# Two further products of the second layer divided once more: a plan of 80 steps on eight banks, with its sums on three engines and DMA

## The chip, the cores and the metric

The kernel runs on one core of a Trainium2 chip. Its time is the device time of one execution in microseconds (us). The core has TensorE (PE, matmuls; PEld are its weight loads), VectorE (DVE), ScalarE (ACT), GpSimd (POOL) and SyncE (SP), each with a queue of its own that is worked off in order, and 16 DMA engines. SBUF is the core's working memory. TensorE writes its results to PSUM, 128 partitions by 8 banks of 512 fp32 numbers; GpSimd and DMA work on SBUF alone here.

## The reference

A causal convolution over 7 tokens with softmaxed weights for each of 8 heads, then a two-layer network with hardswish between its layers:

```python
def _attn_ref(x, weight):            # x: (8, 4096, 192), weight: (8, 7)
    w = np.exp(weight - np.max(weight, axis=-1, keepdims=True))
    w = w / (np.sum(w, axis=-1, keepdims=True) + 1e-09)
    ...
    out = np.einsum('hk,bskhg->bshg', w, x_unf)
    return out.reshape(B, S, D).astype(np.float32)

def _moe_ref(x, w_in, w_out):        # (32768, 192), (192, 2048), (2048, 192)
    h = x @ w_in
    relu6 = np.clip(h + 3.0, 0.0, 6.0)
    g = h * relu6 / 6.0
    return (g @ w_out).astype(np.float32)
```

## The kernel before, in words

The 32,768 tokens are cut into 32 blocks of 1024, each in two halves of 512. A block passes through a convolution (one multiplication on ScalarE, six taps on VectorE, L917-925), the first layer (`first_layer`, L496) and the second (`second_layer`, L589). Block 0 is done in another way (L801-963); blocks 1 to 31 run in the loop at L970. The order of all instructions is written by hand: under `manual_schedule` each engine's queue holds them as the code issues them, and the framework adds the waits.

**First layer.** y is split into three parts, high, low and mix (`split_high`, `split_rest`), and a copy with its halves exchanged is made by six DMAs on SP (`swap_parts`). There are 16 units: for n below 8 group 0 reads the own parts, from 8 on group 1 reads the exchanged ones. `begin(n)` runs the high and low matmuls into a slot of two banks and has ScalarE multiply them by 4097; `end(n)` adds the mix matmuls, ScalarE's relu and VectorE's gate, and then the slot is free. Four slots serve in turn, so begin(n+4) needs gate n. Group 0 writes A11 and A22, group 1 A21 and A12: the four quarters of g, for 8 chunks of 128 rows of the hidden dimension. Taps stand between the gates.

**Second layer.** g @ w_out is one Strassen step over the quarters: seven products P1 to P7, each with a sum of quarters (S1 = A21 + A22, S2 = S1 - A11, S3 = A11 - A21, S4 = A12 - S2) and a sum of weights (T1 to T4). S2 and S1 lie over A11 and A21, S4 over S3. A product has 96 rows, three column groups of 32; TensorE works four such groups at once, and the kernel writes four streams of matmuls, one for each group. `put` books a matmul at its stream's clock, two steps for 512 columns, one for 256; `do(t, ...)` books any other instruction at step t; at the end all are sorted by t and issued. Of P1 and P5 the first two thirds (64 columns) are taken once more by Strassen, over halves of the chunks, of the columns and of the tokens: seven small products of four matmuls in stream 3, with sums Z1 to Z4 (`small_sums`) and weights `w_s` (`small_weights`), 28 steps where the plain form has 32; the last third is run plainly. In this text (n, k) is small product k of P n, or the copy or addition behind it, and Z4 2 is sum 2 for P4. A stream has 82 steps. Three of the four slots are used; the fourth takes begin(0) of the next block's first layer.

**Sums.** P1's Z sums are done by GpSimd during group 0 (L552), S3 by GpSimd and VectorE (L555), two pairs of S1 by DMAs that add in SBUF, issued by GpSimd (L557), the other pairs by VectorE; P5's Z sums by VectorE in A22's place; S2 and S4 by VectorE at step 38. Results c11, c21, c22, c12 are put together on VectorE from PSUM (u3 = U2 + P7 and c21 = u3 + P4 among them), transposed there and stored by SP; c22 and c12 come out at the start of the next block (`finish`). The last block ends with its own order by halves of tokens (`end_lower`, `end_upper`).

Of the kernel before, what the change touches and what calls it, by code (L numbers as in the profile page):

```python
# [8 lines left out]
ALU = mybir.AluOpType  # L9
# [12 lines left out]
HIGH, LOW, MIX = range(3)  # L22


@with_exitstack
def kernel(
# [17 lines left out]
    G = 2  # L44
# [75 lines left out]
    w_s = cst.tile([P, 2, 4, NP // 2, QS], F32, name="w_s")  # L120
# [245 lines left out]

    new_results()
# [34 lines left out]
    def g_sums(engine, which, slots, width):  # L402

        forms = {
            3: (S3, A11, A21, ALU.subtract),
            2: (S2, S1, A11, ALU.subtract), 4: (S3, A12, S2, ALU.subtract),
        }
        for n in which:
            o, a, b, op = forms[n]
            for p in slots[::width]:  # L410
                r = slice(p, p + width)
                engine.tensor_tensor(out=o[:, r], in0=a[:, r], in1=b[:, r], op=op)  # L412
# [75 lines left out]
    y_own, y_other, pools, s1 = [], [None], [], []  # L488

    def swap_parts():  # L490
        y_other[0] = pools[0].tile([P, 3, K3, N], F32, name="y_other", tag="other")
        for n in range(3):
            swap(y_other[0][:, n], y_own[n])


    def first_layer(i, jobs):  # L496
# [6 lines left out]
        def mms(n, part, start=False, stop=False):  # L503
            group, c = divmod(n, NP)
            for s in range(K3):
                for k in range(2):
# [3 lines left out]
                        rhs=r32(y_other[0][r, part, s] if group else y_own[part][r, s]),  # L510
# [30 lines left out]
        for n in range(count):  # L541
# [7 lines left out]
            if n == 1:  # L549
                s1.append(ot.tile([P, NP, N], F32, name="s1", tag="shared")[:])  # L550
            if n < NP and n % 2:
                small_sums(s1[-1], A11, (1, 2, 3, 4), nc.gpsimd, every[n - 1 : n + 1])  # L552
            if n > NP and n % 2:
                pair = slice(n - NP - 1, n - NP + 1)
                g_sums(nc.gpsimd if n + 1 < count else nc.vector, (3,), range(NP)[pair], 2)  # L555
                if n + 3 < count:
                    nc.gpsimd.dma_start(out=S1[:, pair], in_=A22[:, pair], accum_op=ALU.add)  # L557
        for pair in (slice(NP - 2, NP), slice(NP - 4, NP - 2)):
            add(S1[:, pair], A21[:, pair], A22[:, pair])
# [20 lines left out]
    def small_weights(to, w):  # L580

        b11, b12, b21, b22 = (
            w_out[:, c::2, w, q * QS : (q + 1) * QS] for c in range(2) for q in range(2)
        )
        t1, t2, t3, t4 = (to[:, n] for n in range(4))
        for o, p, q in ((t1, b12, b11), (t2, b22, t1), (t3, b22, b12), (t4, b21, t2)):
            nc.gpsimd.tensor_tensor(out=o, in0=p, in1=q, op=ALU.subtract)

    def second_layer(i, between):  # L589
        last = i + 1 == NB  # L590
        ours = [free_slots.pop(0) for _ in range(3)]
        d, e, b, x_, a, c = (psum[:, 2 * n + k] for n in ours for k in range(2))
        ends = [psum[:, 2 * free_slots[0] + k] for k in range(2)] if last else [b, b]
        s5 = A22
        copy = nc.scalar.copy
        m = slice(0, DH)
        lo, hi = halves
        both = nc.sync, nc.scalar
        B, C, V = (bank[rows(3)] for bank in (x_, d, b))
        A, E = e[rows(3)], a[rows(3)]  # L600
        first, second, third, fourth = (rows(q) for q in range(4))
        late = {}
# [17 lines left out]
        def plain(j, bank, n, q, chunks, start=False):  # L620
            x, w = prod[n]
            x = S3 if x is None else x
            for k, ch in enumerate(chunks):
                put(j, 2, lambda ch=ch, k=k: matmul(
                    j, bank[rows(j)], w_out[:, ch, w, q * QS : (q + 1) * QS], x[:, ch],
                    start and k == 0,
                ))

        def small(n, m_, out, start=False):

            x, w = prod[n]
            sums, ws = (s1[-1], w_s[:, 0]) if n == 1 else (s5, w_s[:, 1])
            x11, x12, x21, x22 = four_parts(x)
            z1, z2, z3, z4 = four_parts(sums)
            b11, b12, b21, b22 = (
                w_out[:, h::2, w, q * QS : (q + 1) * QS] for h in range(2) for q in range(2)
            )
            t1, t2, t3, t4 = (ws[:, k] for k in range(4))
            xm, wm = {
                1: (x11, b11), 2: (x12, b21), 3: (z4, b22), 4: (x22, t4),  # L640
                5: (z1, t1), 6: (z2, t2), 7: (z3, t3),
            }[m_]
            for u in range(NP // 2):
                put(3, 1, lambda u=u: matmul(
                    3, out[:, lo], wm[:, u], xm[:, u], start and u == 0
                ))

        def plain_by_halves(j, n, q, t):
            w = prod[n][1]
            for ch in every:  # L650
                put(j, 1, lambda ch=ch: matmul(
                    j, ends[t][rows(j), halves[t]], w_out[:, ch, w, q * QS : (q + 1) * QS],
                    S3[:, ch, halves[t]], ch == 0,
                ))

        def tiles():
            new_results()
            if last:
                xts.insert(0, NP - 1)
            late.update(zip(("p7", "p5", "u3"), (results[0][m, n] for n in range(3))))  # L660

        for q in range(NQ):
            plain(q, d, 4, q, every, True)
            before = (1, 6, NP)[q]
            plain(q, c, 7, q, every[:before], True)
            plain(q, e, 1, 2, range(5 + q, 6 + q))
            do(clock[q], copy, out=e[rows(q + 1)] if q < 2 else p1[third], in_=e[rows(q)])
            plain(q, c, 7, q, every[before:])
            plain(q, a, 2, q, every[:6], True)
            plain(q, b, 6, q, every)  # L670
            plain(q, a, 2, q, every[6:])
            if last:
                plain_by_halves(q, 3, q, 0)
                plain_by_halves(q, 3, q, 1)
            else:
                plain(q, b, 3, q, every)

        def level_two(n, p, chunks, order):
            chunks, first_fill = list(chunks), [True]
            left = [list(chunks) for _ in halves]  # L680

            def fill_half(t, k):
                for _ in range(k):
                    ch = left[t].pop(0)
                    x, w = prod[n]
                    put(3, 1, lambda ch=ch: matmul(
                        3, (ends[0], x_)[t][fourth, halves[t]], w_out[:, ch, w, 2 * QS : 3 * QS],
                        x[:, ch, halves[t]], ch == 0,
                    ))

            def fill(k):
                plain(3, b, n, 2, [chunks.pop(0) for _ in range(k)], first_fill.pop() if first_fill else False)

            steps = {
                1: lambda: copy(out=B[:, lo], in_=A[:, lo]),
                2: lambda: copy(out=p()[first, lo], in_=A[:, lo]),
                6: lambda: copy(out=C[:, lo], in_=B[:, lo]),
                5: lambda: copy(out=p()[second, lo], in_=E[:, lo]),
                7: lambda: add(p()[second, hi], C[:, lo], p()[second, lo]),
# [319 lines left out]
```

## Time and profile before

| what | value |
|---|---|
| runs before | 2228.01, 2227.44, 2227.94 us; median 2227.94 |
| profiled execution, span | 2224.9 us |
| chain that ended last | PE 99%: second layer (L615) 49%, first layer (L508) 46% |
| DMA | 166.57 MB, mean 75 GB/s |
| gates (L306, 128x1024) | x496, 1219 ns each |
| relu (L302, 128x1024) | x496, 1113 ns each |
| 4097 multiplication (L520) | x465, 1008 ns each |
| taps (L921, 128x1536) | x186, 1802 ns each |
| S1 pairs by DMA (L557) | x62, 512 KB each, 5.0 us to landing |

The span counts from the first to the last instruction of one profiled execution; times are of other executions, without a profile. A row of a group gives the line, the engine, the operation, what it writes and reads, the count, the busy time and the mean of one. The chain is followed back from the last instruction, at each step to what released it. A windows row gives a stretch, its length, the busy time of each engine with the count of instructions, TensorE's granted clock (1.00 is full), the DMA engines' busy share and their GB/s. A timeline row gives start, duration, engine, line and operation, and in brackets how long the engine was idle before it and what ended that.

### The profile page before, as it was taken

How to read it: one execution, taken by the hardware profiler on the slowest of the kernel's cores; microseconds unless marked ns; L12 is line 12 of the kernel's file. 1: busy time of each engine (PE TensorE's matmuls, PEld its weight loads, DVE VectorE, ACT ScalarE, POOL GpSimd, SP SyncE). 2: the span in 40 equal slices, each digit the busy share in tenths (PEclk: the TensorE clock that was granted, in tenths of full speed). 3: DMA queues.
4: the chain of work that ended last, by engine and by line, in shares of the span. 5: the costliest groups of instructions: out<-in, count | busy, mean ns of one | idle time of the engine just before them, and what ended most of it. 6: DMA issues, size and time to landing. Idle time of an engine off the chain costs nothing.

```text
span 2224.9 us, 50339 instructions
## 1 busy us (share of the span) xinstructions
PE 2218.0 (100%) x21496; PEld 1532.7 (69%) x21496; DVE 1894.3 (85%) x1673; ACT 1379.2 (62%) x1678; POOL 823.8 (37%) x690
## 2 busy tenths in 40 slices
PE   9999999999999999999999999999999999999999
PEld 5467776677766777766777667776677776677766
DVE  8888888888888888888888888888888888888876
ACT  7457665576655676555766557665567655576654
POOL 2344432344422444223443234442244422344323
PEclk9999999999999999999999999999999999999999
DMA  6244224443244342344422444324434234442232
GB/s 157 57 98 85 49 58 91 85 83 62 53 82 91 77 80 47 71 91 84 85 48 58 91 87 81 67 49 82 91 79 81 47 67 91 84 84 52 55 77 34
DMA packets 253584, 166.57 MB, mean 75 GB/s; under 512 B 208017, under 2 KB 213137, under 8 KB 253361
## 3 DMA queue, kind: packets, MB, share of 16 engines
q1 hardware_dynamic: 234872, 129.46, 28.4%
q0 software_dynamic: 17248, 33.64, 8.7%
q8 instruction: 168, 2.75, 0.5%
q14 instruction: 56, 0.45, 0.1%
q10 hardware_dynamic: 1240, 0.27, 0.1%
HBM read 31.72 MB, written 25.17 MB: 26 GB/s over the span
## 4 chain that ended last, share of the span: by engine, by line
PE 99%; DVE 0%; DMA 0%; ACTq 0%; issue 0%; DVEq 0%; ACT 0%
PE psum L615 49%; PE psum L508 46%; PE psum L296 2%; PE psum L341 2%; DMA x<-in_x_dram 0%; DVE y L255 0%; DVE top L175 0%; ACTq L89 0%; PE psum L816 0%; DVE results L456 0%; DVE scale L171 0%; DVE y L251 0%; DVE scale L192 0%; DVEq L1014 0%; DVE results L462 0%
## 5 line engine op out<-in xcount | busy, mean ns | idle before, releaser
L615 PE MATMUL psum<-g,w_out 128*32 128x512 f32 (+1 forms) x6712 | 967.5, 552 | 0.0
L306 DVE SCALAR_TENSOR_TENSOR g<-g,psum 128x1024 f32<-128x1024 f32 (+1 forms) x528 | 618.3, 1186 | 198.8 <-ACT g L302 194.5
L578 POOL TENSOR_TENSOR s<-g 128x256 f32<-128x256 f32 x248 | 273.6, 1103 | 1241.1 <-DVE g L306 1200.5
L302 ACT ACTIVATE g<-psum,half 128x1024 f32<-128x1024 f32 (+1 forms) x528 | 564.8, 1087 | 6.0 <-PE psum L508 5.2
L615 PEld LDWEIGHTS psum<-g,w_out 128*32 128x32 f32 x6712 | 371.8, 110 | 246.0 <-issue 126.7
L508 PE MATMUL psum<-y,w_in 64*128 64x512 f32 x4464 | 521.4, 388 | 0.0
L508 PE MATMUL psum<-y_other,w_in 64*128 64x512 f32 x4464 | 516.0, 386 | 0.0
L520 ACT ACTIVATE psum<-psum 128x1024 f32<-128x1024 f32 x465 | 469.0, 1008 | 50.7 <-PE psum L508 48.4
L508 PEld LDWEIGHTS psum<-y,w_in 64*128 64x128 f32 x4464 | 413.5, 184 | 115.7 <-issue 26.0
L508 PEld LDWEIGHTS psum<-y_other,w_in 64*128 64x128 f32 x4464 | 418.1, 184 | 87.8
L615 PE MATMUL psum<-s,w_out 128*32 128x512 f32 (+1 forms) x3272 | 465.5, 570 | 0.0
L921 DVE SCALAR_TENSOR_TENSOR y<-x,c_sb,y 128x1536 f32<-128x1536 f32 x186 | 335.2, 1802 | 2.6 <-ACT y L919 1.3
L412 POOL TENSOR_TENSOR s<-g 128x1024 f32<-128x1024 f32 x93 | 285.9, 3074 | 26.2 <-DVE g L306 26.2
L615 PE MATMUL psum<-g,w_s 128*32 128x256 f32 x1240 | 282.8, 379 | 0.0
L615 PEld LDWEIGHTS psum<-s,w_out 128*32 128x32 f32 x3272 | 154.3, 110 | 81.9 <-issue 49.4
L615 PEld LDWEIGHTS psum<-g,w_s 128*32 128x32 f32 x1240 | 136.4, 110 | 67.7
L412 DVE TENSOR_TENSOR s<-g 128x2048 f32<-128x2048 f32 (+1 forms) x93 | 181.3, 1977 | 1.1
L615 PE MATMUL psum<-s,w_s 128*32 128x256 f32 x744 | 170.7, 379 | 0.0
L578 DVE TENSOR_TENSOR g<-g 128x1024 f32<-128x1024 f32 x124 | 151.7, 1224 | 5.3
L412 DVE TENSOR_TENSOR g<-g 128x2048 f32<-128x2048 f32 x62 | 139.1, 2284 | 0.0
L612 ACT COPY psum<-psum 32x512 f32<-32x512 f32 x93 | 51.3, 551 | 135.4 <-PE psum L615 135.4
L456 DVE TENSOR_TENSOR results<-psum,results 32x256 f32<-32x256 f32 (+3 forms) x128 | 69.3, 541 | 50.9 <-issue 45.5
(91 smaller groups left out, 1299.5 us busy)
## 6 DMA issues: line engine op xcount, KB each, us to landing
y_other<-y SPq DMA_DIRECT2D x186, 384.0 KB, 5.1
g<-g POOLq DMA_DIRECT2D x62, 512.0 KB, 5.0
out_dram<-results SPq DMA_DIRECT2D x378, 64.0 KB, 2.0
x<-in_x_dram SPq DMA_DIRECT2D x53, 388.5 KB, 7.7
stage<-in_moe_w_in_dram SPq DMA_DIRECT2D x16, 192.0 KB, 4.5
stage<-in_moe_w_out_dram SPq DMA_DIRECT2D x8, 384.0 KB, 6.8
x<-in_x_dram SPq DMA_DIRECT2D x7, 384.0 KB, 8.4
x<-in_x_dram POOLq DMA_DIRECT2D x2, 388.5 KB, 5.4
```

The costliest lines, as they stand in the source:

```text
L296: nc.tensor.matmul(out=psum[:, b], lhsT=w[r], rhs=src, start=start, stop=stop, skip_group_check=onto,)
L302: nc.scalar.activation(r6, h, ACT.Relu, bias=half[:], scale=1.0 / 6.0)
L306: nc.vector.scalar_tensor_tensor(out=g_, in0=g_, scalar=1.0, in1=h, op0=ALU.min, op1=ALU.mult)
L341: lambda p=p: nc.tensor.matmul(out=bank[j * QS : (j + 1) * QS, tokens], lhsT=w_out[:, p, w, cols], rhs=x[:, p, tokens], start=(first and p ...
L412: engine.tensor_tensor(out=o[:, r], in0=a[:, r], in1=b[:, r], op=op)
L456: nc.vector.tensor_tensor(out=out, in0=x, in1=y, op=op)
L508: nc.tensor.matmul(out=psum[:, 2 * slots[n] + k], lhsT=r32(w_in_parts[part][r, c, s]), rhs=r32(y_other[0][r, part, s] if group else y_own[ ...
L520: nc.scalar.mul(both(n), both(n), 4097.0)
L578: engine.tensor_tensor(out=o, in0=p, in1=q, op=op)
L612: streams[3].append((t - 0.5, lambda: fn(*args, **kw)))
L615: nc.tensor.matmul(out=out, lhsT=w, rhs=x, start=start, stop=True, tile_position=(0, j * QS), skip_group_check=True,)
L921: jobs.append(lambda k=k: nc.vector.scalar_tensor_tensor(out=y[:], in0=x[:, :, k : k + N], scalar=c_sb[:, k : k + 1], in1=y[:], op0=ALU.mu ...
```

## The change

P4 and P7 get the second Strassen step too. The fourth column group (stream 3) now runs 28 small steps each of P1 and P7 and 24 of P5; stream 1 runs P4's 28 and the four of (5, 4), whose result lies aside. Every stream has 80 steps. All four slots are taken. Four steps that write other banks (the last chunks of P5 and P4, and (5, 4)) stand between P6 and P3, which go to the same bank b; in them ScalarE copies b for u3. P4's Z sums are formed with other signs, so that a copy and an adding DMA can make them.

A table, `PLAN`, says for each sum at which step it is issued, and by whom: V VectorE, G GpSimd, D an adding DMA that GpSimd issues after SP or ScalarE has written the first operand. Negative steps lie in the first layer: t belongs to unit int(t + 16). `TIMES` and `ADDS` hold the steps of the other operations. P4's sums lie in the place of the block's own y parts, P7's in that of the exchanged ones (`region`, `sums_in`), P5's where P1's were, and S4 lies over A12 and no longer over S3. Results and transposed results lie in chunks 2 to 7 of A22, so relu and gate of the next block wait for the stores that read there. One tap moves to step 17.3 of the second layer, and the others stand behind units 0, 3 and 11. The exchange of y moves from step 18 to step 64.6, high, low and mix from steps 13 and 15 to steps 46 to 53. Weight sums of four products instead of two are formed at the start by GpSimd. The last block's own order is gone; its stores go to two queues.

```diff
+PLAN = (
+    (-6.74, 'Z4', 1, 'V'),
+    (-6.3, 'S3', 0, 'G'),
+    (-5.2, 'Z4', 2, 'D'),
+    (-3.71, 'S1', 0, 'D'),
+    (-2.66, 'Z4', 3, 'D'),
+    (0.13, 'S3', 3, 'V'),
+    (0.24, 'S3', 1, 'G'),
+    (1.42, 'S3', 2, 'G'),
+    (1.46, 'Z7', 1, 'V'),
+    (2.38, 'Z7', 2, 'V'),
+    (2.47, 'S1', 1, 'D'),
+    (11.07, 'Z7', 3, 'D'),
+    (11.5, 'S1', 2, 'V'),
+    (19.55, 'Z4', 4, 'V'),
+    (22.16, 'Z7', 4, 'D'),
+    (27.2, 'S1', 3, 'V'),
+    (28.62, 'Z5', 3, 'D'),
+    (33.36, 'Z5', 1, 'V'),
+    (34.07, 'S2', 0, 'V', 4),
+    (37.56, 'Z5', 2, 'V'),
+    (41.9, 'Z5', 4, 'D'),
+    (46.42, 'S2', 2, 'V', 4),
+    (49.16, 'S4', 0, 'V', 4),
+    (59.87, 'S4', 2, 'V'),
+    (66.26, 'S4', 3, 'V'),
+)
+TIMES = {'c11': 38.42, 't11': 57.95, 'u3': 60.97, 'c21': 64.27, 't21': 77.97, 'conv6': 17.32, 'high': 46.36, 'low': 47.15, 'mix': 53.24, 'swap': 64.57, 'x': 45.83, 'conv0': 70.49, 'conv1': 70.67, 'a22': 47.43}
+ADDS = {(1, 7): (0, 'V'), (1, 3): (2.43, 'V'), (4, 7): (0.25, 'V'), (4, 3): (1.08, 'V'), (5, 7): (1.83, 'V'), (5, 3): (0.0, 'V'), (7, 7): (0, 'V'), (7, 3): (0, 'V'), (5, 4): (0, 'V'), 'u3': (0, 'G'), 'c22': (0, 'V')}
+CONV_UNITS = (0, 3, 11)
...
-            if n == 1:
-                s1.append(ot.tile([P, NP, N], F32, name="s1", tag="shared")[:])
             if n < NP and n % 2:
-                small_sums(s1[-1], A11, (1, 2, 3, 4), nc.gpsimd, every[n - 1 : n + 1])
-            if n > NP and n % 2:
-                pair = slice(n - NP - 1, n - NP + 1)
-                g_sums(nc.gpsimd if n + 1 < count else nc.vector, (3,), range(NP)[pair], 2)
-                if n + 3 < count:
-                    nc.gpsimd.dma_start(out=S1[:, pair], in_=A22[:, pair], accum_op=ALU.add)
-        for pair in (slice(NP - 2, NP), slice(NP - 4, NP - 2)):
-            add(S1[:, pair], A21[:, pair], A22[:, pair])
+                small_sums(sums[1], A11, (1, 2, 3, 4), nc.gpsimd, every[n - 1 : n + 1])
+            if n == NP - 1:
+                sums[4] = sums_in("own", "sums4")
+                copy_for_sums(sums[4], A22)
+            for t, what, k, by, *width in PLAN:
+                if t < 0 and int(t + count) == n:
+                    sum_of(what, k, by, *width)
+
+    def sum_of(what, k, by, width=2):
+
+        engine = {"V": nc.vector, "G": nc.gpsimd, "D": None}[by]
+        pair = slice(2 * k, 2 * k + 2)
...
+    def copy_for_sums(to, x):
+
+        for k in (1, 2, 3, 4):
+            o, p, q = plus_form(to, x, k)
+            if any(entry[1:4] == ("Z4", k, "D") for entry in PLAN):
+                nc.sync.dma_start(out=o, in_=p)
...
+    def sums_by_dma(to, x, n):
...
+        nc.scalar.mul(o, p, scale)
+        nc.gpsimd.dma_start(out=o, in_=q, accum_op=ALU.add)
...
     def second_layer(i, between):
         last = i + 1 == NB
-        ours = [free_slots.pop(0) for _ in range(3)]
-        d, e, b, x_, a, c = (psum[:, 2 * n + k] for n in ours for k in range(2))
...
+        ours = [free_slots.pop(0) for _ in range(4)]
+        a, A_, E_, C_, B_, b, d, c = (psum[:, 2 * n + k] for n in ours for k in range(2))
...
+        results_in_a22()
+        p7, p5, u3 = (A22[m, k] for k in range(2, 5))
...
+        most, rest = every[: NP - 2], every[NP - 2 :]
+        for q in (0, 2):
+            plain(q, a, 2, q, True)
+        plain(1, a, 2, 1, True, most)
+        plain(0, d, 1, 2, True)
+        do(clock[0], copy, out=b[third], in_=d[first])
+        plain(0, c, 5, 2, True, most)
+        for k in (1, 5, 6, 2, 0, 7, 3, 4):
+            if k:
+                small(1, 4, k)
+                do(33 if k == 2 else ends_at(4, k, clock[1]), step, 4, k)
+            else:
+                plain(1, a, 2, 1, chunks=rest)
+        plain(2, d, 4, 2, True, most)
+        plain(2, c, 7, 2, True)
+        do(clock[2] + 1, copy, out=p7[third], in_=c[third])
+        for q in range(NQ):
+            plain(q, b, 6, q)
+        plain(0, c, 5, 2, chunks=rest)
+        do(clock[0] + 1, copy, out=p5[third], in_=c[first])
+        small(1, 5, 4, aside)
+        do(clock[1] + 1, copy, out=p5[first, hi], in_=aside)
+        plain(2, d, 4, 2, chunks=rest)
+        for q in range(NQ):
+            plain(q, b, 3, q)
+
+        waiting = {(7, 5): TIMES["a22"], (7, 2): TIMES["a22"] + 0.1}
+        for n, k in (
+            [(1, k) for k in (1, 5, 6, 2, 7, 3)] + [(7, 1), (1, 4)]
+            + [(7, k) for k in (5, 6, 2, 7, 3)] + [(5, 1), (7, 4)]
+            + [(5, k) for k in (5, 6, 2, 7, 3)]
+        ):
+            small(3, n, k)
+            do(waiting.get((n, k), ends_at(n, k, clock[3])), step, n, k)
...
+        do(TIMES["c11"], lambda: copy(out=spare["own"][m], in_=b[m]))
+        do(TIMES["c11"] + 0.2, lambda: add(a[m], a[m], spare["own"][m]))
+        for t, what, k, by, *width in PLAN:
+            if t >= 0:
+                do(t, sum_of, what, k, by, *width)
         for t, job in between:
             do(t, job)
...
+        do(TIMES["t11"], lambda: store(i, a, 0, 0))
+        do(TIMES["u3"], lambda: either(u3, b[m], p7, ALU.add, "u3"))
+        do(TIMES["c21"], lambda: add(p7, u3, d[m]))
+        do(TIMES["c21"] + 2 if last else TIMES["t21"], lambda: store(i, p7, 1, 0))
...
-        free_slots.extend(ours[n] for n in (0, 2, 1))
-        if last:
-            end_upper()
+        free_slots.extend(ours[n] for n in (3, 0, 1, 2))
         return [lambda: finish(1), lambda: finish(0)]
```

`either` is an addition on VectorE, or for "G" a copy by ScalarE and an addition by GpSimd. `step(n, k)` is the copy (ScalarE) or addition (VectorE, k = 7 and 3) behind a small product. The small products of P1, P7 and P5 use the same four places in banks A_, E_, B_, C_ one after the other.

## The prediction

> **What bounds the kernel now.** I read the page first, then the chain of waits, then one block of two layers (first layer from 988.77 us, second from 1021.67 us) in the windows, the waits and the timelines of its engines.
>
> ```profile
> PE 2218.0 (100%) x21496; PEld 1532.7 (69%) x21496; DVE 1894.3 (85%) x1673; ACT 1379.2 (62%) x1678; POOL 823.8 (37%) x690
> ...
> 988.77 32.90 PE psum L508 x288
> 1021.67 35.47 PE psum L615 x216
> ...
> 1021.67:1057.14 35.47, 32.73 (x28) 1.00 0.59 119
> 988.77:1021.67 32.90, 25.93 (x23) 1.00 0.16 26
> ...
> DVE g L306 <- ACT g L302: 6.0, 7, 1.2
> ```
>
> TensorE is never idle: the chain is its two layers in turn, 32.90 + 35.47 = 68.37 us for each of 31 blocks. 35.47 us are 82 steps, so a step (256 columns on four column groups) is 0.4326 us. The next engine is VectorE: 25.93 + 32.73 = 58.65 us of 68.37; of the 9.7 us left, 6.0 are gates that wait for ScalarE's relu in the first layer, and can be used only by running late. So TensorE's count sets the time as long as VectorE's queue keeps its dates.
>
> **What the change takes away.** Two steps a block: 2 x 0.4326 = 0.865 us, 26.8 us over 31 blocks. The second layer becomes 80 steps, 34.6 us, the cycle 67.5 us. It has 216 matmuls for 192, but in the last block before, four 256-column matmuls follow each other every 0.21 us, so issuing them sets nothing.
>
> **What it adds, by engine.** VectorE per block: two Z4 and two Z7 sums (1.2 us each, the 128x1024 sums of L578), five more 32x256 additions (0.43); it loses two Z5 sums and u3 (0.69). That is +3.9, so 62.6 of 67.5 us. GpSimd: six more accumulating DMAs (1.20 each) and u3, 25.3 to about 34 us. ScalarE: four scalings of 128x1024 (1.0) and some nine copies (0.36), 42.7 to about 50 us. DMA: six accumulations and two copies of 512 KB more. Sums of busy time fit everywhere; what counts is VectorE's order.
>
> **VectorE's queue, followed by hand.** These rows give the prices, start to start.
>
> ```profile
> 1021.57 3.48 DVE L306 SCALAR_TENSOR_TENSOR g<-g,psum 128x1024 f32<-128x1024 f32 x3 [1.16 <-ACT g L302]
> 1025.08 1.31 DVE L412 TENSOR_TENSOR s<-g 128x1024 f32<-128x1024 f32 x1
> ...
> 1038.21 4.49 DVE L412 TENSOR_TENSOR g<-g 128x2048 f32<-128x2048 f32 x2
> ...
> 1017.74 1.20 POOL L557 DMA_DIRECT2D g<-g  x1 [0.30 <-POOL s L412]
> 1018.49 2.89 POOL L412 TENSOR_TENSOR s<-g 128x1024 f32<-128x1024 f32 x1
> 1021.67 1.20 POOL L557 DMA_DIRECT2D g<-g  x1 [0.30 <-POOL s L412]
> 1022.87 2.43 POOL L412 TENSOR_TENSOR s<-g 128x1024 f32<-128x1024 f32 x1
> ```
>
> The last gate ends 3.4 us into the second layer, and it is paced by ScalarE, so it will again. I count from there: 1.2 for a sum of 1024 elements, 2.2 for 2048, 1.75 for a convolution tap (1.7 for low and mix), 0.45 for a 32x256 addition, 0.7 for 96x512, 0.65 for a transpose.
>
> First, S3's last pair. VectorE's sum started at 1025.08, GpSimd's ended at 1025.30, and VectorE's ended 1.09 after that: one of them waits for the other. In the start-up the same shows the other way round:
>
> ```profile
> 89.08 1.76 DVE L937 TENSOR_TENSOR y<-y,y 128x1536 fp32r<-128x1536 f32 x1 [1.61 <-ACT y L474]
> 90.76 2.01 DVE L477 SCALAR_TENSOR_TENSOR y<-y,y 128x1536 fp32r<-128x1536 f32 x1
> ...
> 88.77 0.65 POOL L83 DMA_DIRECT2D x<-in_x_dram  x1
> 89.43 1.72 POOL L587 TENSOR_TENSOR w_s<-w_out 128x128 f32<-128x128 f32 x1
> 91.22 1.86 POOL L587 TENSOR_TENSOR w_s<-w_out,w_s 128x128 f32<-128x128 f32 x1
> 93.05 0.45 POOL L587 TENSOR_TENSOR w_s<-w_out 128x128 f32<-128x128 f32 x1
> ```
>
> A GpSimd sum of 0.45 us takes 1.72 and 1.86 while VectorE reads two SBUF operands, and then VectorE's 1.75 becomes 2.01. The Trainium skill (SBUF — State Buffer, "Who interferes with whom") has it as an exclusive lock for a VectorE instruction with two SBUF inputs against a GpSimd one that reads SBUF, the first to start keeping it; these rows agree.
>
> Now GpSimd in the changed order: S3's first pair waits for gate 9 (24.7 us into the first layer) and behind it for Z4 1 on VectorE (1.2): 25.9 to 28.3; 0.3 as in the row; three accumulating DMAs (Z4 2, S1 0, Z4 3) 3.6 to 32.2 (an issue keeps the next sum off for its whole 1.2: 2.89 = 0.45 + 2.43); S3 1 and S3 2 2.43 each to 37.06, which is 4.15 into the second layer. Before, it was 3.6. So VectorE's S3 3, ready at 3.4, ends at 4.15 + 1.1 = 5.25 and not at 4.7: 0.55 late, and its whole queue with it. ScalarE's scaling for Z7 3 waits for the same sum; behind it is the copy for (1,6), done at 6.7, due at step 16 = 6.9.
>
> The queue then ends: Z7 1, Z7 2 7.7; S1 2, the last tap and Z4 4 11.85; additions (1,7), (1,3) 12.75; S1 3, Z5 1 15.15; S2's first half 17.35; (4,7) 17.8; Z5 2 19.0; c11, (4,3) 20.15; S2's second half 22.35; low waits 0.3 for ScalarE's high (Z5 4's scaling, two copies and 1.48 of high, begun behind Z5 2) 24.35; (7,7) 24.8; S4's first half 27.0; (7,3) 27.45; mix 29.15; t11 29.8. GpSimd's u3 addition takes 1.3 (half of 2.43 for 512 elements) and holds S4 2 off for 0.65: 31.65; c21 32.35; S4 3 33.55; a tap 35.3; (5,4), (5,7) 36.2; t21 36.85; (5,3) 37.3; the two end results with their transposes 40.0; a tap 41.75; gate 0 42.95; a tap 44.7; gate 1 45.9.
>
> TensorE's dates for the same things: its matmul (1,4) at step 28 = 12.1 us needs (1,7) (12.3): 0.2 late. (4,4) at step 40 = 17.3 needs (4,7): 0.5. (7,4) at step 56 = 24.2 needs (7,7): 0.6. P3 on bank b at step 64 = 27.7 needs ScalarE's copy of b, which stands behind the copy that waits for (7,3): 27.45 + 0.35 + 0.37 + 0.58 = 28.75, so 1.05. The fifth begin of the next layer takes gate 1's bank pair 9.6 us into that layer, 44.2 in this count: 1.7. Late dates don't add up, the largest holds: 1.7 us, of which I take 0.25 back, since ScalarE's gates start from the layer's beginning and have 0.2 to 0.3 us of room against that date. TensorE then waits 1.45 us a block: a cycle of 67.5 + 1.45 = 68.95, 0.58 above 68.37.
>
> **Other edits.** Waits of relu and gates on stores from A22: the last store has its transpose 4 us into the next layer, 1.5 of issue and 2.0 of landing make 7.5, and relu 5 comes at 14: hidden by 6 us. The swap behind t11's stores in SP's queue: six issues took 9.1 us and 5.1 to land, from about 31.5 us, so 9.5 us into the next layer; its first reader comes at 15.8. Sums by DMA: landing 5.0 us (7.4 at most); Z7 4, the tightest, is issued by 11.5 and due at step 48 = 20.8. Eight more weight operations on GpSimd at the start are 4 to 11 us, against 7.2 us of its idle time there: 0 to 4 us, I take 0.5. The plain end: addition, addition, transpose, addition, transpose 3.15 us, issue and landing 3.4, so 6.5 behind the last matmul where it was 2224.9 - 2219.56 = 5.3: +1.2. The last two blocks prepare no further one, which frees 5 us of VectorE: they gain their 0.87.
>
> **The sum**, on the profiled execution: 2224.9 + 29 x 0.58 - 2 x 0.87 + 0.5 + 1.2 = 2241.7. The median of the runs stands 3.0 above that span, so 2244.7; I say 2244. Under 0.2%, 4.5 us, a measurement of this kernel can't tell from no change.
>
> **Rivals.** (A) The cover holds. The lateness is a sum over some forty prices; 0.04 us less on each, or GpSimd's sums done 0.55 us earlier, and every date but the last is met. For it: the dates missed early are missed by 0.2 to 0.6 only, and 6.0 us of gate waits can take up what is left. Below about 0.65 us of waiting a block (68.2) the kernel is faster. With 0.2: 2224.9 - 31 x 0.665 + 1.7 + 3 = 2209; with none 2203. Against it: five dates have no room.
> (B) GpSimd's DMA issue is held off by VectorE too. The tap behind gate 11 (1.75 us) then lies on the Z4 2 issue, S3 2 comes behind VectorE's S3 3 and ends at 7.15, and Z7 1 starts 2.4 late where I counted 0.55: 1.9 us more a block, 2244 + 29 x 1.9 = 2299. Against it: the issue at 88.77 took 0.65 like the one before it, though VectorE's operation at 89.08 lay on its end; only 0.34 us of overlap shows it. The same page of the Trainium skill infers that a tensor_tensor leaves descriptor generation alone; by that rule (B) falls.
> (C) A sum by DMA lands late. Beyond 9 us of landing Z7 4 stops TensorE at step 48; at 12 us for 3 us a block, 2300 or more. Against: 7.4 was the most, at a DMA share of 0.59, and these fall in quieter stretches.
>
> **How the numbers follow.** My forecast, VectorE's queue sets the cycle with 0.65 to 2.2 us of waiting: 0.50, of which 0.06 lie within 0.2% and 0.44 above. (A) 0.35, of which 0.02 within. (B) 0.11, (C) 0.04. Faster 0.33, within 0.08, slower 0.59. The forecast's own range is 2222 to 2267. For 8 in 10 I go down to 2203, (A) without any wait, and up to 2282, short of (B) and (C) in full.
>
> **What would show it.** Right: the cycle near 69 us, TensorE idle at step 64 and at the fifth begin, there behind a gate; VectorE busy over 90% with no wait between gates 0 and 3; S3 3 prolonged by GpSimd's S3 2; u3 longer than 1.3 us or S4 2 longer than 1.2. Wrong: a second layer of 34.6 us and a first of 32.9; or waits on sums that a DMA brings; or an accumulating issue well over 1.2 us while VectorE runs a tap.

## The result, and the profile after

The changed kernel takes 2258.4 us (median of 4 runs, 2258.27 to 2258.60), the kernel before 2228.0 in the same comparison: a ratio of 1.0137, 95% interval 1.0122 to 1.0151. It is slower by 30 us.

The page of the changed kernel, its engines; then one block in windows (first layer from 1142.17 us, second from 1175.84; the columns are the stretch, its length, the busy time of PE, PEld, DVE, ACT and POOL with their counts, the granted clock, the DMA share and GB/s).

```profile
PE 2240.0 (99%) x22920; PEld 1622.9 (72%) x22920; DVE 2034.1 (90%) x1884; ACT 1577.5 (70%) x2049; POOL 1041.6 (46%) x910
```

```profile
1142.17:1175.84 33.67, 33.67 (x293) 27.51 (x289) 28.60 (x26) 30.68 (x31) 21.46 (x21) 1.00 0.56 115
1175.84:1211.46 35.62, 35.41 (x433) 23.81 (x432) 34.63 (x32) 18.35 (x33) 11.15 (x8) 1.00 0.87 149
```

By its steps alone the second layer falls from 35.47 us to 34.6 and the first stays at 32.90, and the prediction put 1.45 us of waiting on top of the two; they are 35.62 and 33.67. VectorE has 28.60 + 34.63 = 63.23 us of work in a block of 69.29. The mean over the blocks is 69.32, against 68.38 before, and 30 blocks of 0.94 more are 28 us of the 32 by which the spans differ (2256.8 against 2224.9). The page still says 99% for TensorE, where it said 100% before: waits of half a microsecond hardly show there. They show in the waits of its weight loads, over the whole run (us in total, times, longest).

```profile
PEld psum L721 <- ACT g L770: 20.8, 30, 0.7
PEld psum L721 <- ACT g L783: 13.8, 30, 0.5
...
PEld psum L553 <- DVE g L338: 11.8, 29, 0.8
PEld psum L553 <- DVE psum L569: 11.3, 30, 0.4
```

Thirty times each, so once a block: at step 64 of the second layer P3 waits for the copy of bank b for u3 (L770); at step 52 small product (5, 1) waits for the copy of (7, 2) out of its bank (L783); in the first layer begin(5), which the prediction calls the fifth (units count from 0), waits for gate 1 (L338), and the last mix matmuls for VectorE's half of the last multiplication by 4097 (L569). VectorE's queue is behind all four: here is its timeline from the end of the first layer to the middle of the second, and around gate 1.

```profile
1175.34 3.48 DVE L338 SCALAR_TENSOR_TENSOR g<-g,psum 128x1024 f32<-128x1024 f32 x3 [0.45 <-ACT g L334]
1178.86 1.39 DVE L449 TENSOR_TENSOR s<-g 128x1024 f32<-128x1024 f32 x1
1180.35 1.23 DVE L643 TENSOR_TENSOR sums<-s 128x1024 f32<-128x1024 f32 x1
...
1200.29 2.29 DVE L449 TENSOR_TENSOR g<-g 128x2048 f32<-128x2048 f32 x1
1202.61 0.43 DVE L493 TENSOR_TENSOR g<-psum,g 32x256 f32<-32x256 f32 x1
...
1215.50 1.77 DVE L1004 SCALAR_TENSOR_TENSOR y<-x,c_sb,y 128x1536 f32<-128x1536 f32 x1
1217.20 1.21 DVE L338 SCALAR_TENSOR_TENSOR g<-g,psum 128x1024 f32<-128x1024 f32 x1
1218.33 1.81 DVE L1004 SCALAR_TENSOR_TENSOR y<-x,c_sb,y 128x1536 f32<-128x1536 f32 x1
1220.06 2.34 DVE L338 SCALAR_TENSOR_TENSOR g<-g,psum 128x1024 f32<-128x1024 f32 x2
```

Brackets (idle time) are what to look for: between 1175.34 and 1222.4 the whole answer has only one more, 0.25 us in front of low. But for that, VectorE works for 47 of 69 us without a gap. S3 3 (1178.86) takes 1.39 us where its later neighbours take 1.23, under GpSimd's S3 2. The addition of (7, 3) at 1202.61 stands behind S4's first half (1200.29), though TensorE had ended small product (7, 3) some 22.7 us into the layer, near 1198.5. Behind the addition ScalarE copies for (5, 1), and behind that it copies bank b, which is what TensorE waits for at step 64.

### The profile page after: what moved, and what is told of

It is laid out like the page before. It is cut to its first block, busy times and chain, and to the rows that moved or that the text cites. A ratio compares the mean times of both kernels' runs of the same rounds, so it can differ in the third digit from the quotient of the medians.

```text
span 2256.8 us, 54880 instructions
## 1 busy us (share of the span) xinstructions
PE 2240.0 (99%) x22920; PEld 1622.9 (72%) x22920; DVE 2034.1 (90%) x1884; ACT 1577.5 (70%) x2049; POOL 1041.6 (46%) x910
## 5 line engine op out<-in xcount | busy, mean ns | idle before, releaser
L721 PE MATMUL psum<-g,w_out 128*32 128x512 f32 (+1 forms) x7440 | 1079.2, 550 | 6.3 <-ACT g L770 6.3
L338 DVE SCALAR_TENSOR_TENSOR g<-g,psum 128x1024 f32<-128x1024 f32 (+1 forms) x528 | 616.1, 1184 | 158.7 <-ACT g L334 156.3
L553 PE MATMUL psum<-y_own,w_in 64*128 64x512 f32 x4464 | 531.2, 391 | 1.0 <-DVE g L338 0.7
L553 PEld LDWEIGHTS psum<-y_own,w_in 64*128 64x128 f32 x4464 | 415.7, 184 | 111.5 <-issue 13.2
L721 PE MATMUL psum<-sums,w_s 128*32 128x256 f32 x1984 | 459.6, 379 | 0.0
L721 PE MATMUL psum<-sums,w_out 128*32 128x256 f32 x1984 | 458.2, 379 | 0.0
L643 POOL TENSOR_TENSOR sums<-g 128x256 f32<-128x256 f32 x248 | 227.7, 918 | 490.4 <-DVE g L338 428.7
L449 DVE TENSOR_TENSOR g<-g 128x2048 f32<-128x2048 f32 (+1 forms) x155 | 298.2, 1924 | 1.9
L721 PEld LDWEIGHTS psum<-sums,w_out 128*32 128x32 f32 x1984 | 218.1, 110 | 78.3 <-issue 0.2
L721 PE MATMUL psum<-s,w_out 128*32 128x256 f32 (+1 forms) x992 | 272.8, 486 | 0.0
L721 PEld LDWEIGHTS psum<-sums,w_s 128*32 128x32 f32 x1984 | 215.8, 110 | 58.6
L675 POOL DMA_DIRECT2D sums<-g x62 | 79.4, 1281 | 204.5 <-DVE psum L493 120.1
```

The costliest lines, as they stand in the source:

```text
L338: nc.vector.scalar_tensor_tensor(out=g_, in0=g_, scalar=1.0, in1=h, op0=ALU.min, op1=ALU.mult)
L553: nc.tensor.matmul(out=psum[:, 2 * slots[n] + k], lhsT=r32(w_in_parts[part][r, c, s]), rhs=r32((y_other if group else y_own)[0][r, part, s ...
L643: engine.tensor_tensor(out=o, in0=p, in1=q, op=op)
L675: nc.gpsimd.dma_start(out=o, in_=q, accum_op=ALU.add)
L721: nc.tensor.matmul(out=out, lhsT=w, rhs=x, start=start, stop=True, tile_position=(0, j * QS), skip_group_check=True,)
```

## The experiments

Twelve kernels, made from the changed one. Times are medians; each ratio is against the kernel before (2226.6 to 2226.7 us in these comparisons). "Cycle" is the mean of a block over the run, first and second layer together: 69.32 us in the changed kernel.

### First round: is it the amount of VectorE's work?

The theory T was that VectorE's queue sets the cycle at all four dates, so that work taken from it comes back one for one.

**Taps off the dates.**

```diff
-CONV_UNITS = (0, 3, 11)
+CONV_UNITS = (1, 5, 7)
```

> The three taps of the first layer follow gates 1, 5 and 7 instead of 0, 3 and 11; nothing else is changed. Theory T (VectorE's ordered queue, 63.2 us of work in a block of 69.29, sets the cycle at four dates: step 52, step 64, the begin of multiplication 5, the last 4097 multiplication): both first-layer waits (0.33 and 0.34 us a block) go, and about half of it comes back at the two dates of the second layer, since the gates after 7 now run behind the taps; cycle 68.9 to 69.0, 2245 to 2252 us against 2258.4. Rival D (the load of the DMA engines, 0.87 in the second layer, sets the cycle) and rival L (GpSimd and VectorE excluding each other): no change, 2256 to 2261 us, since neither DMA nor GpSimd work moves.

Measured: 2273.1 us, ratio 1.021 (1.0194 to 1.0225): 15 us slower than the changed kernel. The first layer fell as foretold, to 33.11; the second rose to 36.76, by 1.1 and not 0.3. Its timeline of VectorE says why:

```profile
2091.28 3.48 DVE L338 SCALAR_TENSOR_TENSOR g<-g,psum 128x1024 f32<-128x1024 f32 x3 [1.16 <-ACT g L334]
2094.79 2.07 DVE L449 TENSOR_TENSOR s<-g 128x1024 f32<-128x1024 f32 x1
```

All three taps now lie beside GpSimd's Z1 sums of the first layer, where one did. Each makes a sum of 0.74 us take 2.24 to 2.26, GpSimd's S3 comes later, and S3 3, which follows gate 15, takes 2.07 us instead of 1.39 and ends 1.1 us later in the layer. Everything behind it is 1.1 late, and TensorE waits 0.33 and 0.83 us for the additions (1, 7) and (4, 7) (L493) at steps 28 and 40, where it had not waited for them. So nothing in the second layer's first half has room, and D and L as I had put them (no change) fall too: who runs beside whom is part of a tap's price.

**A sum by DMA instead of VectorE.**

```diff
-    (11.5, 'S1', 2, 'V'),
+    (2.5, 'S1', 2, 'D'),
```

> S1 2 is added by an accumulating DMA issued right behind that of S1 1 instead of by VectorE: VectorE loses 1.15 us at s+11.5, the DMA engines gain 512 KB. Theory T: every later date has VectorE 1.15 us earlier, the cycle falls by 0.9 to 1.15 us to 68.1 to 68.4, 2223 to 2231 us. Rival D: the DMA engines have 2 to 3.5 us more work a block, so the time rises to over 2265 us and the transfers land later. Rival L: GpSimd's additions are unchanged, so the time stays within 4 us of 2258.

Measured: 2283.1 us, ratio 1.0255 (1.0238 to 1.0272), 25 us slower: rival D's direction. VectorE did lose its 1.2 us. The window of one second layer, the transfers of the Z7 and Z5 sums (GpSimd's issues), and TensorE's wait in that block:

```profile
2029.49:2066.76 37.27, 35.84 (x433) 23.11 (x433) 33.67 (x31) 18.43 (x33) 12.89 (x9) 1.00 0.97 165
```

```profile
DMA to landing us min/median/max: 5.4/11.4/15.5
```

```profile
2050.51 0.14 PEld L721 LDWEIGHTS psum<-sums,w_s 128*32 128x32 f32 x2 [1.93 <-ACT g L718]
```

The same run's waits of TensorE itself, in total:

```profile
PE psum L721 <- DMA sums<-s: 27.9, 32, 1.9
```

One accumulation of 512 KB more takes the DMA share from 0.87 to 0.97. Landing of the Z7 and Z5 sums, a median of 7.5 us and 10.3 at most in the changed kernel, becomes 11.4 and 15.5. In this block Z7 3 was issued at 2035.35 and landed at 2050.41; TensorE's step on that sum began at 2050.51, after 1.93 us idle. The bracket names a ScalarE copy that had long ended; it is the DMA, as TensorE's own total has it. The changed kernel has no such line. So DMA doesn't set the cycle of the changed kernel, but it has less than one such sum of room, and VectorE can't be relieved there.

**A tap left out, and a tap done twice.**

```diff
-            between = [(TIMES["conv6"], job) for job in final]
+            between = []
```

> The last tap of the convolution (conv6, 1.75 us of VectorE in the second layer) is left out, so y lacks one of its taps; nothing else is changed. Theory T: VectorE has 61.5 us of work a block and the cycle falls one for one until few waits are left: by 1.4 to 1.75 us to 67.5 to 67.9, 2204 to 2215 us. Rivals D and L: under 5 us of gain, since DMA and GpSimd do the same work.

> The same tap is done twice, so y holds it twice: 1.75 us more of VectorE at the same place. Theory T: one for one, the cycle rises by 1.6 to 1.9 us to 70.9 to 71.2, 2307 to 2318 us. Rivals D and L: under 20 us more, the work hides beside the waits.

(The second of the two books the job at conv6 and again 0.05 steps later.) Measured: 2242.2 us without the tap (ratio 1.007, 1.0055 to 1.0085), 2313.4 with two (one run). One tap more costs 55 us, 1.8 a block, one for one as T has it; one less gives 16 us, 0.5 a block, where T wanted 1.4 at least. And of the four waits only that of step 52 is gone (without the tap):

```profile
PEld psum L721 <- ACT g L770: 20.8, 30, 0.7
...
PEld psum L553 <- DVE g L338: 11.6, 29, 0.8
PEld psum L553 <- DVE psum L569: 11.3, 30, 0.4
```

The same kernel's VectorE, 8 to 12 us into a second layer:

```profile
2001.50 1.22 DVE L664 TENSOR_TENSOR sums<-g,sums 128x1024 f32<-128x1024 f32 x1
2002.77 0.44 DVE L493 TENSOR_TENSOR psum<-psum,sums 32x256 f32<-32x256 f32 x1
2004.44 0.44 DVE L493 TENSOR_TENSOR psum<-psum,sums 32x256 f32<-32x256 f32 x1 [1.24 <-ACT psum L785]
2004.91 1.22 DVE L612 TENSOR_TENSOR g<-g 128x1024 f32<-128x1024 f32 x1
```

Of the 1.8 us freed VectorE spends 1.24 waiting in front of an addition of small products (the bracket names a ScalarE copy that itself waits for TensorE), and goes on 0.6 us earlier than in the changed kernel; from there to gate 1 the order is as it was. T falls: not the amount of VectorE's work sets the cycle but a chain. Theory C: TensorE from the fifth begin, held by gate 1, to the last units of the first layer; from gate 13 VectorE's queue without a gap, through the second layer, to gate 1 of the next. An addition 11 us into the second layer ties the two together, so that less work ahead of it soon gains nothing.

### Second round: does a wait removed come back?

**S4's first half behind (7, 3)**; **a tap behind gate 1**; **both**.

```diff
-    (49.16, 'S4', 0, 'V', 4),
+    (52.2, 'S4', 0, 'V', 4),
...
-CONV_UNITS = (0, 3, 11)
+CONV_UNITS = (1, 3, 11)
```

> S4 0 (2.29 us of VectorE) is put behind the (7,3) addition instead of ahead of it, so that the copy of (5,1) and the copy of b for u3 come earlier; no work is added or removed. Theory C (after the first runs: one chain sets the cycle, TensorE from multiplication 5 of the first layer to (4,7) 11 us into the second, then VectorE's queue without a gap from there to gate 1): the wait at step 64 (0.69 us a block) goes, the same 0.6 to 0.7 us come back at gate 1, whose wait grows from 0.37 to about 1.0 us; 2255 to 2262 us, no change against 2258.4. Rival S (the waits are separate sums, each removed one is gained): 0.69 x 30 = 21 us less, 2236 to 2240 us.

> One tap of the first layer follows gate 1 instead of gate 0; nothing else is changed. Theory C: gate 1 ends 1 us before it is waited for, the wait for it (0.37 us a block) goes, and nothing gives it back, since gates 4 and on have the same starts; cycle 68.9, 2246 to 2249 us. Rival F (VectorE's work alone sets the cycle, so that a wait only moves): within 3 us of 2258.

> Both edits of the two runs before. Theory C: with the tap off gate 1, gate 1 has 1 us to spare, so the 0.69 us of step 64 are now gained as well; waits fall by 0.37 + 0.65, cycle 68.2 to 68.4, 2225 to 2232 us: more than the sum of the two edits by themselves. Rival S: the sum of the two, whatever they gave by themselves.

Measured: 2256.5 us (ratio 1.0134, 1.0119 to 1.0149), 2252.9 (1.0118, 1.0102 to 1.0133) and 2241.3 (1.0065, 1.005 to 1.008). In gains on the changed kernel: 1.9, 5.5, and 17.1 together, more than twice their sum. The waits of the first of the three:

```profile
PEld psum L553 <- DVE g L338: 23.0, 32, 0.9
...
PEld psum L721 <- ACT g L783: 13.7, 30, 0.5
...
PEld psum L553 <- DVE psum L569: 11.2, 30, 0.4
```

Step 64's line is gone, and gate 1's has doubled from 11.8 to 23.0: the second layer is 0.43 shorter (35.21), the first 0.37 longer (34.06). That is C, and rival S falls. With a tap taken out of the stretch before gate 1 the same edit is worth its 0.4. The sizes were under what I wrote, and both kernels with the tap moved lie above C's range: the removed wait of 0.69 shortened the layer by 0.43 only (perhaps a wait shown at one weight load holds some of the spacing that the matmuls have anyway; no run tests that), and the tap behind gate 1 runs beside GpSimd, which makes the one behind gate 3 longer (2.15 us for 1.98) and gate 4 late, a new wait of 0.2.

**All four taps into the first layer**, behind gates 1, 3, 7 and 10, with S4 as above.

```diff
-            ahead = conv[:-1]
-            jobs = {n: [job] for n, job in zip(CONV_UNITS, ahead[-3:])}
-            jobs[-1] = left + ahead[:-3]
+            jobs = {n: [job] for n, job in zip(CONV_UNITS, conv[-4:])}
+            jobs[-1] = left + conv[:-4]
```

> S4 0 behind (7,3), and all four taps that were left (three in the first layer, one in the second) in the first layer, behind gates 1, 3, 7 and 10, where VectorE idles 0.8 us a gate; the same work. Theory C: the waits of gate 1 (0.37), of the last 4097 multiplication (0.38), of step 64 (0.69) and of step 52 (0.46 + 0.2) all go, if GpSimd, which the two middle taps hold off by some 1.5 us each, still ends its S3 by 3.4 us into the second layer; TensorE is left without a wait, cycle 67.5 to 67.8, 2206 to 2215 us, under the kernel before (2227). Rival L (GpSimd and VectorE holding each other off): S3 and its sums come over 0.7 us later, and the second layer gives back over 0.7 us a block, 2230 us or more.

Measured: 2295.0 us (2289 to 2301), ratio 1.03 (1.0276 to 1.0324), slower than any other kernel with the same work. The second layer is 34.68 us and has no wait of note left; the first has a mean of 36.0. Gate 11 was 2.2 us late, behind this tap:

```profile
1607.60 1.63 DVE L664 TENSOR_TENSOR sums<-g 128x1024 f32<-128x1024 f32 x1
1609.15 1.21 DVE L338 SCALAR_TENSOR_TENSOR g<-g,psum 128x1024 f32<-128x1024 f32 x1
1610.28 2.83 DVE L1004 SCALAR_TENSOR_TENSOR y<-x,c_sb,y 128x1536 f32<-128x1536 f32 x1
1613.03 2.34 DVE L338 SCALAR_TENSOR_TENSOR g<-g,psum 128x1024 f32<-128x1024 f32 x2
```

```profile
1607.40 0.75 POOL L643 TENSOR_TENSOR sums<-g,sums 128x256 f32<-128x256 f32 x1
1608.10 3.40 POOL L449 TENSOR_TENSOR s<-g 128x1024 f32<-128x1024 f32 x1
1611.43 1.29 POOL L662 DMA_DIRECT2D sums<-sums  x1
1612.21 1.73 POOL L610 DMA_DIRECT2D g<-g  x1
1612.93 2.33 POOL L662 DMA_DIRECT2D sums<-g  x1
1614.33 3.33 POOL L449 TENSOR_TENSOR s<-g 128x1024 f32<-128x1024 f32 x1
1619.99 2.39 POOL L449 TENSOR_TENSOR s<-g 128x1024 f32<-128x1024 f32 x1 [2.34 <-ACT g L334]
```

GpSimd's S3 0 had begun at 1608.10 and ran to 1611.50; the tap of 1.8 us, ready at 1610.28, ended 1.6 us after that, 2.83 in all. And I had the date wrong: the last begin stands ahead of end(13), so gate 11 is due 0.7 us sooner than the rhythm of the others says. Rival L's mechanism, but at another place than either theory had named.

The wait is not all of it. Two first layers of this run in windows of TensorE (length, busy time, granted clock, DMA share, GB/s):

```profile
1582.80:1619.53 36.73, 34.94 (x289) 0.95 0.60 123
1725.63:1760.73 35.10, 33.31 (x289) 1.00 0.58 119
```

In both, TensorE runs nothing for 1.79 us ahead of the last begin. In the first the granted clock of the next 4 us is 0.66, in the second 1.00. The profiled execution has the drop in 16 of its blocks, at 1.6 us each: 26 of its 2297 us. At full clock the layer is 35.1, which is the 2.2 us of gate 11 over 32.95. What decides between the two is open: a halt of 1.90 us in the run with one sum more by DMA has no drop behind it, and the other runs' mean clock is 0.998 or more.

### Third round: VectorE's stretch before gate 1 made shorter

**The c22 addition on GpSimd**, c12 finished first; alone and with the four taps behind gates 0, 3, 7 and 11. S4 stays behind (7, 3) in all four kernels of this round. In the two with this addition c12 is written over P5's part before c22 is added, so c22 holds u3 + c12.

```diff
-... 'c22': (0, 'V')}
+... 'c22': (0, 'G')}
...
-        return [lambda: finish(1), lambda: finish(0)]
+        return [lambda: finish(0), lambda: finish(1)]
```

> S4 0 behind (7,3), as before, and the addition for c22 (0.69 us of VectorE between the layers) on GpSimd, idle there, with c12 finished first; the taps as in the changed kernel. Theory C: VectorE's queue before gate 1 is 0.69 us shorter, which takes the whole of the wait for gate 1, the one that step 64 gave back included down to about 0.05 us, and leaves gate 4 at its date; the waits of step 52 (0.46 + 0.2) and of the last 4097 multiplication (0.37) stay; cycle 68.2 to 68.4, 2225 to 2232 us, against 2241.3 with the tap moved. If GpSimd's addition comes late for the second transpose, gate 1 waits again and the time is 2240 us or more.

> The same with all four remaining taps in the first layer, behind gates 0, 3, 7 and 11: none is left in the second layer, and none meets GpSimd's S3 0, which held the tap behind gate 10 for 2.83 us. Theory C: TensorE has no wait left in the second layer (34.7 us) and only that of the last 4097 multiplication (0.37) and 0.2 in the first (33.2 to 33.4); cycle 67.9 to 68.1, 2215 to 2222 us, less than the kernel before (2226.7). Rival L (GpSimd, held off 1.5 us more by the tap behind gate 7, ends its S3 late): the second layer keeps waits of 0.5 us or more at step 28 and the time is over 2230 us.

Measured: 2254.9 us (ratio 1.0127, 1.0111 to 1.0142) and 2240.1 (1.0061, 1.0048 to 1.0073). For the first, the case that I had put last came, and in both the addition waits for c12's, and the transpose for the addition (lines of the second):

```profile
1478.21 0.71 DVE L499 STREAM_TRANSPOSE g<-g 96x512 f32<-96x512 f32 x1
1479.64 0.71 DVE L499 STREAM_TRANSPOSE g<-g 96x512 f32<-96x512 f32 x1 [0.72 <-POOL g L853]
1480.27 1.77 DVE L1004 SCALAR_TENSOR_TENSOR y<-x,c_sb,y 128x1536 f32<-128x1536 f32 x1
```

0.69 us saved, 0.72 waited. The taps did what C says of them: the second layer of the other kernel is 34.68 in most blocks, without a wait. The first, with gate 1 still late (a wait of 0.71), is 34.0, so the time lies above C's range and past the mark that I had set for L, but without L's waits in the second layer.

**c12 into the bank of b, and a tap ahead of c22's transpose**; and a variant with the taps earlier still.

```diff
-            if k:
-                engine = nc.vector if ADDS["c22"][1] == "V" else nc.gpsimd
-                engine.tensor_tensor(out=u3, in0=u3, in1=p5, op=ALU.add)
-            else:
-                add(p5, b[m], p5)
-            store(i, u3 if k else p5, k, 1, queues=both if last else (nc.sync,))
+            if not k:
+                nc.gpsimd.tensor_tensor(out=u3, in0=u3, in1=p5, op=ALU.add)
+                add(b[m], b[m], p5)
+            store(i, u3 if k else b, k, 1, queues=both if last else (nc.sync,))
...
+CONV_UNITS = (0, 3, 7, 11)
+            jobs[-1] = left[:1] + conv[:-4] + left[1:]
```

> As the run before, but c12 is added into the bank of b, so that GpSimd's c22 addition needs nothing of it, and the tap between the layers is put ahead of the transpose of c22, so that VectorE has work while GpSimd adds (it waited 0.72 us for GpSimd in the run before, which gave the gain back); taps behind gates 0, 3, 7 and 11, S4 0 behind (7,3). Theory C: gate 1 ends before it is waited for; second layer 34.7 to 35.0, first 33.2 to 33.4 us, cycle 67.9 to 68.3, 2215 to 2227 us. Rival F (VectorE's amount of work sets the cycle, wherever it stands): 2236 us or more, since only 0.69 us of it is gone and the rest has been moved.

> The same, with the transpose of c22 behind gate 0, two taps between the layers, and the others behind gates 1, 5 and 7: no tap behind gate 11, so the last 4097 multiplication is not held. Theory C: its wait (0.37) goes too; VectorE's S3 3 ends 1 us later in the second layer, as in the first run with these taps (GpSimd's Z1 and S3 held off), but the second layer no longer has a tap and takes that; first layer 32.9 to 33.2, second 34.7 to 34.9, cycle 67.6 to 68.1, 2207 to 2221 us. If the lateness of S3 3 decides: the second layer waits 0.3 us or more at the additions of P4, 2225 us or more.

Measured: 2221.2 us (9 runs, 2220.05 to 2222.05), ratio 0.9975 (0.9966 to 0.9985), and 2235.4, ratio 1.004 (1.0026 to 1.0053). The first is 37 us under the changed kernel and 5.4 (0.25%) under the kernel before: faster than both, and in C's range. The second is above C's. A block of it in windows (second layer, then first):

```profile
1496.75:1531.43 34.68, 34.68 (x433) 25.79 (x432) 33.14 (x30) 18.54 (x33) 12.58 (x8) 1.00 0.90 157
1531.43:1564.73 33.30, 33.30 (x289) 30.22 (x289) 29.88 (x27) 30.55 (x31) 23.79 (x22) 1.00 0.55 116
```

and the waits that are left:

```profile
PEld psum L553 <- DVE psum L569: 7.7, 30, 0.3
...
PEld psum L721 <- ACT g L783: 1.3, 4, 0.4
```

VectorE has 33.14 + 29.88 = 63.02 us of work, as good as the 63.23 of the changed kernel, in 67.98 us instead of 69.29. Rival F falls by this: it is the order. In the variant the second layer is 34.82 although S3 3 takes 2.1 us again (the layer without a tap takes that up, as C says), and L569 waits no more; but with two taps between the layers and others behind gates 1 and 7, gates 0, 2 and 8 are late (waits of 0.35, 0.62 and 0.21), and the first layer is 33.76.

## Why the prediction was right, and where its steps were off

**Slower, by VectorE's dates: right.** I gave 2244 and a cycle of 68.95; it is 2258 and 69.32. Two steps a block are indeed gone: the second layer without waits is 34.68 in three of the kernels (34.6 predicted), and the first 32.95 in every last block, which prepares none. Of the signs that I had named, TensorE waits at step 64 and behind gate 1 at begin(5), VectorE is busy for 91% of the block (with one wait that I had not named, 0.41 us in front of gate 3), S3 3 is prolonged, u3's addition takes 1.51 us and S4 2 1.55.

**Amount of work: right.** VectorE 62.6 of 67.5 predicted, 63.23 measured; GpSimd 34 and 32.6; ScalarE 50 and 49.0.

**S3's last pair: right, against a layer that had become longer.** GpSimd's queue in the last third of the first layer and the start of the second (the first row is S3 0, which VectorE's Z4 1 holds off at its start):

```profile
1167.30 3.32 POOL L449 TENSOR_TENSOR s<-g 128x1024 f32<-128x1024 f32 x1 [1.12 <-DVE g L338]
1170.56 1.29 POOL L662 DMA_DIRECT2D sums<-sums  x1
1171.33 1.73 POOL L610 DMA_DIRECT2D g<-g  x1
1172.06 2.33 POOL L662 DMA_DIRECT2D sums<-g  x1
1172.85 6.30 POOL L449 TENSOR_TENSOR s<-g 128x1024 f32<-128x1024 f32 x2
```

I had S3 2 end 37.06 us after the first layer's start; it ended after 36.98 (1179.15). S3 3 ended 1.1 us behind it, as foretold, and took 1.39 us in place of 1.23. The issues cost GpSimd what I had taken: from 1170.56 the three and the two sums behind them take 8.59 us, 3.6 + 4.86 foretold. But the second layer started 0.77 us later than I had it, because TensorE waits in the first layer too, so that S3 2 ended 3.31 us into the second layer and not 4.15. The three early dates (steps 28, 40, 56, foretold 0.2 to 0.6 late) were therefore met, but for 0.2 at step 40. With taps elsewhere VectorE and GpSimd holding each other off cost 0.7 us more (S3 3 at 2.07).

**Step 64: right in kind.** 1.05 foretold, 0.69 seen, worth 0.43 of the layer's length.

**"Late dates don't add up, the largest holds": right. The 0.25 given back: the step that failed.** From begin(5) of one block to gate 1 of the next I had 78.8 - 9.6 = 69.2 us; the trace has 69.23 (1152.03 to 1221.27). That is closer than the steps between: from gate 9 to S3 2 I had 12.4 us for 11.9, and from S3 3 to gate 1 40.65 for 41.0, two errors that cancel by luck. TensorE itself needs 34.68 + 32.95 = 67.63 us, so it waits 1.7 us a block, the 1.7 of my largest date. It waits in several places and not at gate 1 alone: the second layer is 0.95 longer than without waits, and gate 1 and L569 hold the first by some 0.37 each. The 0.25 that I took back for ScalarE's room does not show: 0.25 x 29 = 7 of the 14 us. Another 0.12 a block, 3 us, is what the cycle of 69.32 has over 69.2. That the waits of step 52 and L569 would come back at gate 1 if they alone went is argued from C, and was shown for step 64 only. Two things speak for it: VectorE does not wait for TensorE behind gate 13, and the last relu starts at 1176.20, right behind the one before it and 0.36 us after TensorE's last matmul of the layer, so that L569 does not seem to delay a gate.

**Start and end.** The first of the blocks has a first layer of 35.8 us, 2.1 over the others, for 0.5; the tail after the last matmul is 7.2 us for 6.5. The gain of 0.87 came in the last block alone, not in two. These are most of the rest; against them the median stands 1.6 us above the span and not 3.0.

**Rivals.** (A), the cover holds: it does not in this order, and it does nearly in another (2221; I gave 2209 for 0.2 us of waiting left, and this has 0.46 over the 67.6 without waits). (B), issues held off by VectorE: not so, though the sign that I had named for it is there: with the tap behind gate 11 beside them the issues have rows of 1.29, 1.73 and 2.33 us. But they have the same rows where no tap lies beside them (1.29, 1.73 and 2.33 in the run with taps behind gates 1, 5 and 7), those of L675 take 1.28 to 1.29 us with VectorE sums beside them, and S3 2 came when it was due. (C), late DMA: not in the changed kernel, whose Z7 and Z5 sums land within 10.3 us and where TensorE waited for a DMA once in these blocks; the run with one sum more by DMA shows how near it is.

**Open.** Not tried: an order with no wait at all (67.6 a block), and which of the added sums could be done by fewer instructions. Which part of the 2.1 us at the start is due to the weight sums was not separated.

## What to carry to other kernels

When one engine's queue is busy without a gap over most of a cycle, find where the gap is and what ties its two ends to the engine that counts; work added inside the stretch counts one for one (1.8 us for a tap), work taken out only until TensorE's next result is what the queue waits for (0.5 for a tap), a wait inside the stretch is worth nothing until the stretch is shorter, and work moved into the gap is free only if it meets no date and no neighbour there. So test edits in pairs: two that give 2 and 5 us by themselves gave 17 together. And where VectorE and GpSimd both read SBUF, an instruction's price depends on what runs beside it, so a queue that was balanced by fixed durations shifts when an operation is moved.

## What was not expected of the hardware

VectorE can be the one that waits, and for long. The run with a tap behind gate 10 shows a whole chain of it: VectorE's Z4 1 (1607.60) lies on the end of a GpSimd sum (1607.40) and takes 1.63 us, where it takes 1.22 with GpSimd idle; GpSimd's S3 0 (1608.10) starts inside Z4 1 and takes 3.40, where one beside gates alone takes 2.39 (1619.99); the tap (1610.28) starts inside S3 0 and takes 2.83. The gate between them, which reads one operand from PSUM, takes its 1.21. The Trainium skill (SBUF — State Buffer, "Who interferes with whom") has it that whichever of the two issues first keeps the port and that the other is blocked; these rows agree. What I had not seen is that the blocks pass on, from one engine to the other and back, so that one sum of 0.75 us too late costs three instructions their time.

An accumulating DMA's issue on GpSimd has rows of 1.3 to 2.3 us, and what follows starts 0.73 to 0.79 us after it (1170.56, 1171.33, 1172.06, 1172.85 in the changed kernel). The rows overlap, so neither their lengths nor their starts tell what the queue loses; the end of the sum behind them does. From 1170.56 to 1179.15 are 8.59 us; two sums of 2.39 leave 3.81, or 1.27 an issue. In the run with a tap behind gate 10 the sum behind the three issues starts 0.6 us later against them and its row is 3.33, but from 1611.43 to 1617.66 are 6.23 us, and one sum leaves 3.84: 1.28 an issue.

The DMA engines had little room: at a share of 0.87 the Z7 and Z5 sums land after a median of 7.5 us, at 0.97 after 11.4, for one accumulation more beside eight a block. Whether the load or the place in the queue behind the added transfer does it was not separated.

A wait can cost TensorE more than its length: with the same 1.79 us without a matmul, the granted clock of the next 4 us was 0.66 in one block and 1.00 in another, and the layer 36.73 or 35.10 us.
